# The second mixture's first product by Strassen's seven half products, over blocks of 768 tokens

## The chip, the cores and the metric

One core of a Trainium2 chip runs the whole program. The metric is the device time of one execution in microseconds (us), the median of several runs. TensorE (PE) multiplies and sums into PSUM, VectorE (DVE), ScalarE (ACT) and GpSimd (POOL) work elementwise, and SyncE (SP) issues most of the DMA transfers.

## What is computed

```python
x = attention(q, k, v, s)        # B=4, H=8, S=576, D=64, causal, with a cumulative bias -> 2304 tokens x 512
h = x @ w_in1;  x1 = (h * sigmoid(1.702 * h)) @ w_out1      # first mixture:  512 -> 2048 -> 512
h = x1 @ w_in2; r = maximum(h, 0)
out = (s2 * (r * r) + b2) @ w_out2                          # second mixture: 512 -> 2048 -> 512
```

All of it is float32. TensorE's float32 operands here are of the rounded kind (fp32r), so each product is made of three: an operand is split into a high part (a copy to fp32r) and a low part (the operand less its high part), and low x high, high x low and high x high are summed in PSUM.

## The kernel before

The 2048 hidden columns are 16 slices of 128, numbered f. Weights come from DRAM as pairs of 32-bit words, 512 KB for one f of `w_in` or `w_out` (`fetch_w`, the DMA at L125), are joined to floats (`join_w`: ACT at L139, DVE at L140 and L141) and split (`split_w`: ACT at L149, DVE at L150). The first part of the program runs the attention heads on TensorE among the first mixture's products (L404 for h, L444 for y), unit by unit; the first batch's attention heads run while the first mixture's weights are being loaded, and what order the vector engines take there is set by the scheduler of the language from the program's order and the buffers (only TensorE's order, and SP's in part, is written out by hand).

The last unit of the first mixture, 256 tokens, is `first_whole`: for each f twelve matmuls of 256 columns make h (L404), ACT, DVE, ACT and POOL turn it into two parts (L425, L426, L430, L431), and four f later twelve matmuls add them into four y sums (L580). Beside it the first weights of the second mixture are joined and split. `second` then goes over four blocks of 512 tokens and one of 256: for each f, `h2` sums twelve matmuls 128x512 (L554) in one PSUM bank, three banks in turn; ACT takes the positive part (L557), DVE squares it (L558) and applies s and b (L559), ACT makes the high part (L562), and the low part is made at L563 by POOL where f is even, by DVE where it is odd. Two f later (LEAD2) twelve matmuls at L604 add into four y sums, one for each 128 tokens. All weights of the second mixture stay in SBUF, split, after block 0 has brought them. `fetch_x` and `parts_x` load and split the tokens of a block (ACT at L544, POOL at L545) during the block ahead. In the second mixture the order of PE is by hand everywhere, that of ACT and DVE up to the end of block 0.

Of the kernel before, what the change touches and what calls it, by code (L numbers as in the profile page):

```python
# [17 lines left out]
P = 128  # L18
# [4 lines left out]
ACT, DVE = mybir.EngineType.Activation, mybir.EngineType.DVE  # L23
# [12 lines left out]
WIDE2, LEAD2, PLACES, FETCHED = 512, 2, 9, 5  # L36
# [31 lines left out]
def fused_kernel(ctx: ExitStack, tc: tile.TileContext, qkT, vP, s, w1i, w1o, w2i, w2o, s2, b2, out):  # L68
# [59 lines left out]
    def join_w(came):  # L128

        if came.dtype == F32:  # L130
            return came
        else:

            lower, upper = came[:, 0 : 2 * CM : 2], came[:, 1 : 2 * CM : 2]
            nc.scalar.activation(f32(upper), f32(upper), AF.Prelu, scale=2.0**-112, alpha=2.0**32)  # L139
            nc.vector.tensor_scalar(out=lower, in0=lower, scalar1=2.0**-29, scalar2=7.49, op0=ALU.mult, op1=ALU.min)  # L140
            nc.vector.scalar_tensor_tensor(  # L141
                out=lower, in0=upper, scalar=3, in1=lower, op0=ALU.logical_shift_left, op1=ALU.bitwise_or
            )
            return f32(lower)

    def split_w(single, tag, f):

        w = wp.tile([P, 2, CM], F32R, tag=tag, name=f"{tag}{f}")
        nc.scalar.activation(w[:, 0, :], single, AF.Copy)  # L149
        nc.vector.tensor_tensor(w[:, 1, :], single, f32(w[:, 0, :]), ALU.subtract)  # L150
        return w

    def load_w(stage, src, tag, f):
        return split_w(join_w(fetch_w(stage, src, f)), tag, f)


    with ExitStack() as p1:
        sp = p1.enter_context(tc.tile_pool(name="sp", bufs=8))
# [252 lines left out]
        def h_begin(ui, f, x):  # L411
            ph = begun[ui, f] = psM.tile([P, 512], F32, tag="m", name="ph1")
            for _ in h_sum(ph, units[ui].n, f, x, range(len(x))):
                pass

        def h_item(ui, f, x, between=None):
            n = units[ui].n
            if (ui, f) in begun:
                ph = begun.pop((ui, f))
                yield from h_sum(ph, n, f, x, range(NC - 1, NC))  # L420
            else:
                ph = psM.tile([P, 512], F32, tag="m", name="ph1")
                yield from h_sum(ph, n, f, x, range(NC))
# [72 lines left out]
        with tc.tile_pool(name="half0", bufs=1) as pool, tc.manual_schedule(engines={PE}):  # L496
            attention_pool(pool, B * H, 0)
            x0 = []
            with tc.manual_schedule(engines={PE, SP}):
                setup()  # L500
                for step in range(H + 2):
# [7 lines left out]
                    for f in range(len(wi), min(NF, 2 * step)):  # L509
                        wi[f] = load_w((wp, "wo", NF), w1i, "wi", f)  # L510
# [12 lines left out]
        with tc.tile_pool(name="half1", bufs=1) as pool, tc.manual_schedule(engines={PE}):  # L523
# [6 lines left out]
    rawp = ctx.enter_context(tc.tile_pool(name="rawp", bufs=PLACES))  # L530
    psY = ctx.enter_context(tc.tile_pool(name="psY", bufs=5, space=PSUM))
    xp2 = ctx.enter_context(tc.tile_pool(name="xp2", bufs=2))
    wi2, wo2 = {}, {}
    blocks = [(t, min(WIDE2, NT - t)) for t in range(0, NT, WIDE2)]

    def fetch_x(t0, n, cc):
        raw = xp2.tile([P, WIDE2], F32, tag="xraw2", name="xraw2")
        nc.sync.dma_start(raw[:, :n], x1_d[cc * P : (cc + 1) * P, t0 : t0 + n])
        return raw

    def parts_x(raw, n):

        x = rawp.tile([P, 2, WIDE2], F32R, tag="pair", name="xT2")
        nc.scalar.activation(x[:, 0, :n], raw[:, :n], AF.Copy)  # L544
        nc.gpsimd.tensor_tensor(x[:, 1, :n], raw[:, :n], f32(x[:, 0, :n]), ALU.subtract)  # L545
        return x

    def h2(f, x, n, g2, between):
        ph = psM.tile([P, 512], F32, tag="m", name="ph2")
        k = 0  # L550
        for cc in range(NC):
            wc = slice(cc * P, (cc + 1) * P)
            for a, b in ((1, 0), (0, 1), (0, 0)):
                nc.tensor.matmul(ph[:, :n], wi2[f][:, a, wc], x[cc][:, b, :n], start=(k == 0), stop=(k == 3 * NC - 1))  # L554
                k += 1
        r = xp.tile([P, 2 * NMAX], F32, tag="xT", name="r")[:, :n]
        nc.scalar.activation(r, ph[:, :n], AF.Relu)  # L557
        nc.vector.tensor_tensor(r, r, r, ALU.mult)  # L558
        nc.vector.tensor_scalar(out=r, in0=r, scalar1=s_sb, scalar2=b_sb, op0=ALU.mult, op1=ALU.add)  # L559
        between()  # L560
        g = [gp.tile([P, 2 * NMAX], F32R, tag="g", name="g2")[:, :n] for _ in range(2)]
        nc.scalar.activation(g[0], r, AF.Copy)  # L562
        (nc.vector if f % 2 else nc.gpsimd).tensor_tensor(g[1], r, f32(g[0]), ALU.subtract)  # L563
        g2[f] = g
# [28 lines left out]
    def second(t0, n, x, last):  # L593
        g2 = {}
        py = [psY.tile([P, C], F32, tag="y", name="py2") for _ in range(n // P)]
        for f in range(NF + LEAD2):
            if f < NF:
                h2(f, x, n, g2, join_next)
                yield f
            if f >= LEAD2:  # L600
                k = f - LEAD2
                for t in range(n // P):
                    for i, (a, b) in enumerate(((1, 0), (0, 1), (0, 0))):
                        nc.tensor.matmul(  # L604
                            py[t], g2[k][a][:, t * P : (t + 1) * P], wo2[k][:, b, :],
                            start=(k == 0 and i == 0), stop=(k == NF - 1 and i == 2),
                        )
        for t in range(n // P):
            y = xp2.tile([P, C], F32, tag="y2", name="y2", bufs=3)
            if last and t == n // P - 1:  # L610
                half = C // 2
                for i, (copy, queue) in enumerate(((nc.scalar.copy, nc.scalar), (nc.vector.tensor_copy, nc.sync))):
                    mine = slice(i * half, (i + 1) * half)
                    copy(y[:, mine], py[t][:, mine])
                    queue.dma_start(out[t0 + t * P : t0 + (t + 1) * P, mine], y[:, mine])
                continue
            if t % 2:
                nc.scalar.activation(y, py[t], AF.Copy)
            else:
                nc.vector.tensor_copy(y, py[t])  # L620
            nc.sync.dma_start(out[t0 + t * P : t0 + (t + 1) * P, :], y)

    order = sorted(
# [87 lines left out]
```

## Time and profile before

| | |
|---|---|
| runs | 1056.04, 1053.0, 1053.21 us; median 1053.21 us |
| profiled execution, span | 1052.8 us (its own time is not listed apart) |
| granted TensorE clock | 0.995 |
| PE busy | 1015.6 us, 96% of the span, 6216 matmuls |
| DVE / ACT / POOL busy | 650.6 / 535.8 / 347.7 us |

Busy time is the time in which an engine has an instruction running; a matmul's time in the trace is its own from start to end, and as matmuls overlap, the pace is read from a run of them (time divided by count). Idle time in square brackets stands before an instruction, with what released it. The program's stretches by time: attention and first mixture to 606 us, `first_whole` to 652 us, then blocks 0 to 4 of `second` from 652, 750, 837, 924 and 1011 us.

### The profile page before, as it was taken

To read this page: it belongs to the slowest core of one execution; us is meant where nothing else is said; L and a number is where in the kernel's file an instruction comes from. 1 tells how busy PE (TensorE), PEld (TensorE's weight loads), DVE (VectorE), ACT (ScalarE), POOL (GpSimd) and SP (SyncE) were. 2 spreads that over 40 slices of the span, in tenths; PEclk is the share of its full clock that TensorE was granted. 3 is DMA by queue.
4 is the path that set the end of the run, shared out by engine and by line. 5 is a ranking of instruction groups with operands and counts; after the bars stand their busy time and mean duration, and the time that the engine had idled before them with its cause. 6 is when DMAs were issued, how large, how long until landed. Compare 5 with 4: busy or idle time off the path is not lost.

```text
span 1052.8 us, 17330 instructions
## 1 busy us (share of the span) xinstructions
PE 1015.6 (96%) x6216; PEld 909.6 (86%) x6216; DVE 650.6 (62%) x1441; ACT 535.8 (51%) x1252; POOL 347.7 (33%) x382
## 2 busy tenths in 40 slices
PE   5989999999999999999999999999999999999998
PEld 3459989999989999999999999788888888888887
DVE  4689877567467788778877579866422332232343
ACT  4888856646536646656656557544422322222222
POOL 1126535435335436435445235112410301111011
PEclk9998999999999999999999999999999999999999
DMA  5665331221042232222222084531300100100010
GB/s 178 217 236 182 120 97 56 65 81 44 6 129 71 67 105 72 83 92 72 84 74 68 21 300 134 167 101 41 110 1 1 65 1 1 46 1 1 1 40 21
DMA packets 39181, 85.51 MB, mean 81 GB/s; under 512 B 5660, under 2 KB 16536, under 8 KB 39096
## 3 DMA queue, kind: packets, MB, share of 16 engines
q1 hardware_dynamic: 38888, 84.27, 25.1%
q8 instruction: 49, 0.80, 0.3%
q14 instruction: 36, 0.29, 0.1%
q10 hardware_dynamic: 208, 0.13, 0.0%
HBM read 70.29 MB, written 10.03 MB: 76 GB/s over the span
## 4 chain that ended last, share of the span: by engine, by line
PE 78%; DVE 11%; ACT 4%; DMA 3%; issue 2%; SPq 1%; DVEq 0%; ACTq 0%
PE py L604 19%; PE ph L554 18%; PE py L444 14%; PE ph L404 14%; PE ps L277 4%; PE pst L315 4%; PE po L342 3%; DVE hi L115 3%; DMA pair<-w1i 2%; DVE x L283 1%; PE py L580 1%; ACT x L289 1%; DVE pair L141 1%; DVE pair L140 1%; PE po L336 1%
## 5 line engine op out<-in xcount | busy, mean ns | idle before, releaser
L404 PE MATMUL ph<-xT,wi 128*128 128x320 f32 (+1 forms) x1536 | 246.1, 305 | 5.6 <-ACT xT L390 2.5
L404 PEld LDWEIGHTS ph<-xT,wi 128*128 128x128 f32 x1536 | 217.0, 193 | 7.1 <-ACT xT L390 3.0
L444 PE MATMUL py<-g,wo 128*128 128x320 f32 (+1 forms) x1344 | 215.2, 304 | 0.0
L604 PE MATMUL py<-wo,g 128*128 128x512 f32 x864 | 208.1, 390 | 2.4 <-POOL g L563 2.4
L554 PE MATMUL ph<-xT,wi 128*128 128x512 f32 (+1 forms) x960 | 208.4, 368 | 0.0
L554 PEld LDWEIGHTS ph<-xT,wi 128*128 128x128 f32 x960 | 169.0, 188 | 31.0
L604 PEld LDWEIGHTS py<-wo,g 128*128 128x128 f32 x864 | 161.1, 188 | 36.2 <-POOL g L563 3.3
L444 PEld LDWEIGHTS py<-g,wo 128*128 128x128 f32 x1344 | 188.0, 189 | 0.9 <-POOL g L431 0.2
L558 DVE TENSOR_TENSOR r<-r 128x512 f32<-128x512 f32 (+1 forms) x80 | 53.6, 670 | 189.1 <-ACT r L557 188.9
L431 POOL TENSOR_TENSOR g<-th,g 128x320 fp32r<-128x320 f32 (+1 forms) x128 | 116.3, 909 | 128.9 <-ACT g L430 114.2
L563 POOL TENSOR_TENSOR g<-r,g 128x512 fp32r<-128x512 f32 (+1 forms) x40 | 48.6, 1216 | 306.3 <-PE py L604 174.9
L289 ACT ACTIVATE x<-x,m 64x64 f32<-64x64 f32 (+2 forms) x160 | 89.5, 560 | 100.2 <-DVE m L283 98.8
L557 ACT ACTIVATE r<-ph 128x512 f32<-128x512 f32 (+1 forms) x80 | 44.4, 555 | 147.7 <-PE ph L554 146.1
L257 POOL TENSOR_TENSOR lo<-raw,hi 64x576 fp32r<-64x576 f32 (+1 forms) x56 | 68.1, 1217 | 123.0 <-issue 57.2
L283 DVE CUSTOM_DVE_ANT_0 x<-ps,mask 64x64 f32<-64x64 f32 (+2 forms) x160 | 68.1, 426 | 52.2 <-PE ps L277 50.4
L315 PE MATMUL pst<-ident,x 128*128 128x128 f32 (+2 forms) x480 | 85.8, 287 | 9.9 <-DVE ph L324 8.1
L562 ACT ACTIVATE g<-r 128x512 fp32r<-128x512 f32 (+1 forms) x80 | 47.1, 589 | 91.9 <-DVE r L559 91.8
L113 POOL TENSOR_SCALAR x<-x,tot 64x64 f32<-64x64 f32 (+1 forms) x96 | 49.3, 520 | 91.3 <-DVE tot L294 71.4
L321 ACT ACTIVATE ph<-pst 64x256 fp32r<-64x256 f32 (+2 forms) x144 | 67.0, 473 | 20.6 <-PE pst L315 19.2
L315 PEld LDWEIGHTS pst<-ident,x 128*128 128x128 f32 (+2 forms) x480 | 54.8, 136 | 24.7 <-DVE ph L324 13.0
L425 ACT ACTIVATE th<-ph 128x320 f32<-128x320 f32 (+1 forms) x128 | 51.7, 404 | 45.5 <-PE ph L404 42.7
L426 DVE SCALAR_TENSOR_TENSOR th<-th,ph 128x320 f32<-128x320 f32 (+1 forms) x128 | 57.5, 449 | 22.5 <-ACT th L425 21.5
(71 smaller groups left out, 1334.8 us busy)
## 6 DMA issues: line engine op xcount, KB each, us to landing
raw<-qkT SPq DMA_DIRECT2D x32, 416.0 KB
pair<-w1o SPq DMA_DIRECT2D x16, 512.0 KB
pair<-w1i SPq DMA_DIRECT2D x16, 512.0 KB
pair<-w2i SPq DMA_DIRECT2D x16, 512.0 KB
pair<-w2o SPq DMA_DIRECT2D x16, 512.0 KB
raw<-qkT SPq DMA_DIRECT2D x24, 320.0 KB
vraw<-vP SPq DMA_DIRECT2D x16, 320.0 KB
out<-y SPq DMA_DIRECT2D x17, 256.0 KB
```

The costliest lines, as they stand in the source:

```text
L257: nc.gpsimd.tensor_tensor(lo[:D, kc], raw[:D, kc], f32(hi[:D, kc]), ALU.subtract)
L283: nc.vector.tensor_tensor_reduce(out=x[:w, j0:j1], in0=ps[:w, : j1 - j0], in1=mask[:w, WIDE - a0 + j0 : WIDE - a0 + j1], scale=-1.0 / ROOT ...
L289: nc.scalar.activation(x[:w, :a1], x[:w, :a1], AF.Exp, bias=least, scale=-1.0, accum_out=tot[:w, c : c + 1])
L315: nc.tensor.transpose(ps[: j1 - j0, at : at + a1 - a0], t["x"][c][: a1 - a0, j0:j1], ident[: a1 - a0, : a1 - a0])
L321: nc.scalar.activation(t["ph"][:rows, base:end], ps[:rows, :m], AF.Copy)
L404: nc.tensor.matmul(ph[:, :n], wi[f][:, a, cc * P : (cc + 1) * P], x[cc][:, b, :n], start=(k == 0), stop=(k == 3 * NC - 1),)
L426: nc.vector.scalar_tensor_tensor(out=th[:, :n], in0=th[:, :n], scalar=1.0, in1=ph[:, :n], op0=ALU.add, op1=ALU.mult)
L431: nc.gpsimd.tensor_tensor(g[:, 1, :n], th[:, :n], f32(g[:, 0, :n]), ALU.subtract)
L444: nc.tensor.matmul(py[:, :n], wo[f][:, a, wc], g_t[ui, f][:, b, :n], start=(k == 0), stop=(k == 3 * G - 1))
L554: nc.tensor.matmul(ph[:, :n], wi2[f][:, a, wc], x[cc][:, b, :n], start=(k == 0), stop=(k == 3 * NC - 1))
L558: nc.vector.tensor_tensor(r, r, r, ALU.mult)
L604: nc.tensor.matmul(py[t], g2[k][a][:, t * P : (t + 1) * P], wo2[k][:, b, :], start=(k == 0 and i == 0), stop=(k == NF - 1 and i == 2),)
```

## The change

The second mixture takes its tokens in three blocks of 768 (two halves of 384, `HALF2`), and its first product by Strassen's scheme for 2 x 2 blocks. The blocks of the weights are `w_in2` for one pair of slices (f even, f odd) by two halves of the 512 inputs, those of the tokens two halves of the inputs by two halves of the block. Seven half products take the place of eight: each is 6 matmuls of 128 x 384 (two 128-deep slices of inputs, three terms each). A step p is one pair of slices, so a block has 8 steps.

The work around it:
- `product` (L687) sums into three banks. Slots 0, 2, 4 and 5 of a step add one after another into one bank, `sum_p`, and ACT copies the partial sum out (`taken`, L735) after slots 0, 2, 4 and 5 before the next of them goes on. Slot 1 has the bank `sum_q`, slots 3 and 6 have `sum_r`. DVE adds the copies to `sum_q` and `sum_r` as it reads them (`added`, L738). `squared` (DVE, L741, 768 columns), `affine` and `high` (ACT, L744 and L748) and `low` (L751, DVE for even f, POOL for odd f) make the two parts.
- y of a step is 36 matmuls of 512 columns (L702), which stand 5 or 6 at a time behind each slot, from step 1's slot 3 on (`LAG2`).
- The weight blocks: POOL forms the sums of a pair (`sums_of`, L604, four operations of 256 columns), ACT and DVE split the operands (`parts_of`, L620 and L621: three of 512 and one of 256 columns). Block 0 writes these parts, 1.83 MB for a step, to DRAM (L622), and blocks 1 and 2 read them back (L614).
- The tokens: DVE forms differences (L641, L642) and ACT with DVE or POOL splits them (L647, L648); a table, `X_WORK`, sets beside which slot. For block 0 this stands in the loop around `first_whole`.
- The order of PE, ACT, DVE and POOL is by hand from `first_whole` to the end. Buffers of `wp` have a tag each, and the pool ranges of the attention lie on the other side of SBUF.

```diff
+    N2, W = HALF2, 2 * P
+    NP, T2, N_BLOCKS = NF // 2, 2 * HALF2 // P, NT // (2 * HALF2)
+    parts_d = dram.tile([NP, 4, P, 4 * W], F32, name="parts_d")
...
+    def sums_of(p):
+        w, t = whole[p], wp.tile([P, 4, W], F32, tag="wi7", name="sums")
+        a11, a12, a21, a22 = (w[:, f, k * W : (k + 1) * W] for f in range(2) for k in range(2))
+        for to, a, b, op in (
+            (t[:, 1], a21, a22, ALU.add), (t[:, 0], t[:, 1], a11, ALU.subtract),
+            (t[:, 2], a11, a21, ALU.subtract), (t[:, 3], a12, t[:, 0], ALU.subtract),
+        ):
+            nc.gpsimd.tensor_tensor(to, a, b, op)
...
+    def parts_of(p, k, first):
...
+        if not first:
+            nc.sync.dma_start(flat, kept)
+            return
...
+        nc.scalar.activation(t[:, 0, :], src, AF.Copy)
+        nc.vector.tensor_tensor(t[:, 1, :], src, f32(t[:, 0, :]), ALU.subtract)
+        nc.sync.dma_start(kept, flat)
...
-    def second(t0, n, x, last):
...
+    PRODUCTS = (
+        ("p", 0, 0, "11"), ("q", 0, 1, "21"), ("p", 1, 0, "2"), ("r", 1, 1, "1"),
+        ("p", 2, 0, "3"), ("p", 3, 0, "4"), ("r", 2, 1, "22"),
     )
+    def product(ps, p, slot, x):
+        _, group, at, kind = PRODUCTS[slot]
+        w, first = parts[p, group], slot in (0, 1, 3)
+        for k in range(6):
+            a, b = ((1, 0), (0, 1), (0, 0))[k % 3]
+            c0 = at * W + k // 3 * P
+            nc.tensor.matmul(
+                ps[:, :N2], w[:, a, c0 : c0 + P], x[kind, k // 3][:, b, :], start=(first and k == 0), stop=(k == 5),
+                skip_group_check=not first,
+            )
...
+            for slot, (bank, _, _, _) in enumerate(PRODUCTS):
+                if slot in (0, 1, 3):
+                    ps[bank] = psM.tile([P, 512], F32, tag="m0" if slot == 0 else "m1", name="sum_" + bank)
+                product(ps[bank], p, slot, x)
+                if slot == 0:
+                    taken(e[0], "p")
...
+                elif slot == 1:
+                    added(even[:, :N2], "q", e[0])
...
+                elif slot == 4:
+                    taken(e[2], "p")
+                    added(odd[:, N2:], "r", e[2])
+                elif slot == 5:
+                    taken(odd[:, :N2], "p")
+                elif slot == 6:
+                    squared(odd)
+                    added(even[:, N2:], "r", e[1])
...
+                beside(p, slot)
+                if step > 1 or (step == 1 and slot >= LAG2):
+                    y_next(6 if slot == 4 else 5)
```

The order of TensorE changes only from the end of `first_whole` on. There it was, before, twelve matmuls for each f (`ph` is the sum of one f, `py` a sum of y):

```order
L554 MATMUL ph_8892<-xT_8644,wi_8362 128x512 x3
L554 MATMUL ph_8892<-xT_8647,wi_8362 128x512 x3
L554 MATMUL ph_8892<-xT_8732,wi_8362 128x512 x3
L554 MATMUL ph_8892<-xT_8735,wi_8362 128x512 x3
L604 MATMUL py_8830<-wo_8401,g_8855 128x512
L604 MATMUL py_8830<-wo_8401,g_8854 128x512 x2
L604 MATMUL py_8831<-wo_8401,g_8855 128x512
```

And it is now, from step 1's slot 2 to the y matmuls behind its slot 5:

```order
L687 MATMUL sum_p<-xs,part 128x384 x6
L687 MATMUL sum_r<-xs,part 128x384 x6
L702 MATMUL py_8988<-wo_8495,g_8913 128x512 x3
L702 MATMUL py_8988<-wo_8454,g_8953 128x512 x2
L687 MATMUL sum_p<-xs,part 128x384 x6
L702 MATMUL py_8988<-wo_8454,g_8953 128x512
L702 MATMUL py_9013<-wo_8495,g_8913 128x512 x3
L702 MATMUL py_9013<-wo_8454,g_8953 128x512 x2
L687 MATMUL sum_p<-xs,part 128x384 x6
L702 MATMUL py_9013<-wo_8454,g_8953 128x512
L702 MATMUL py_9033<-wo_8495,g_8913 128x512 x3
L702 MATMUL py_9033<-wo_8454,g_8953 128x512
```

On TensorE step 0 and step 1's slots 0 to 2 have no y matmuls between them; later each slot has five or six behind it.

The first eleven rows of DVE's step 2, in block 0, as they now stand ( `whole` is a pair of weight slices, `part` its split operands, `g` the parts of the hidden values):

```order
L738 TENSOR_TENSOR even<-sum_q,e 128x384
L154 TENSOR_SCALAR pair<-pair 128x512
L156 SCALAR_TENSOR_TENSOR whole<-pair 128x512
L621 TENSOR_TENSOR part<-whole,part 128x512
L751 TENSOR_TENSOR g_9099<-even,g_9099 128x768
L621 TENSOR_TENSOR part<-sums,part 128x512
L154 TENSOR_SCALAR pair<-pair 128x512
L156 SCALAR_TENSOR_TENSOR pair<-pair 128x512
L738 TENSOR_TENSOR odd<-sum_r,e 128x384
L165 TENSOR_TENSOR wo_9159<-pair,wo_9159 128x512
L621 TENSOR_TENSOR part<-sums,part 128x512
```

The whole step has 20 DVE operations: four joins of two operations each, two `wo` splits, four part splits (three of 512 columns, one of 256), three `added`, two `squared` and one `low`; POOL has four `sums_of` operations of 256 columns and one `low` of 768.

The other place is far ahead of the change, in the first batch's attention, where the scheduler sets the order. SP's transfers stood there so (`w1i` and `w1o` are the first mixture's weights, 512 KB each; `raw` and `vraw` belong to the attention heads):

```order
L125 DMA pair<-w1i 128x1024 x2
L237 DMA raw<-qkT 64x640
L233 DMA raw<-rows_d 4x320
L234 DMA raw<-rows_d 4x320
L244 DMA vraw<-vP 128x384
L125 DMA pair<-w1i 128x1024 x2
```

And now:

```order
L133 DMA pair<-w1i 128x1024 x2
L254 DMA raw<-qkT 64x640
L250 DMA raw<-rows_d 4x320
L251 DMA raw<-rows_d 4x320
L133 DMA pair<-w1o 128x1024 x3
L261 DMA vraw<-vP 128x384
L133 DMA pair<-w1i 128x1024 x2
```

Seven `w1o` slices are loaded, joined and split ahead of most of the attention heads of the first batch, between them, where they came behind before. TensorE's own order in this stretch is the same. DVE there, before and now, at the same place (L283 and L300 are the same mask operation of a head):

```order
L141 SCALAR_TENSOR_TENSOR pair<-pair 128x512
L283 ISA x,m<-ps,mask 128x320
L283 ISA m 128x1
L140 TENSOR_SCALAR pair<-pair 128x512
L150 TENSOR_TENSOR wi_280<-pair,wi_280 128x512
L141 SCALAR_TENSOR_TENSOR pair<-pair 128x512
```

```order
L165 TENSOR_TENSOR wo_689<-pair,wo_689 128x512
L300 ISA x,m<-ps,mask 128x320
L300 ISA m 128x1
L154 TENSOR_SCALAR pair<-pair 128x512
L156 SCALAR_TENSOR_TENSOR pair<-pair 128x512
L165 TENSOR_TENSOR wi_280<-pair,wi_280 128x512
```

A `wo` split has come in ahead of the head's mask operation, and six more follow within the next hundred rows.

## Rows read from the trace of the kernel before

**Rows 1.** The page: busy us (share) x instructions; chain by engine.
```profile
PE 1015.6 (96%) x6216; PEld 909.6 (86%) x6216; DVE 650.6 (62%) x1441; ACT 535.8 (51%) x1252; POOL 347.7 (33%) x382
...
PE 78%; DVE 11%; ACT 4%; DMA 3%; issue 2%; SPq 1%; DVEq 0%; ACTq 0%
```

**Rows 2.** Chain of waits in order of time: start us, duration us, what.
```profile
613.57 1.44 PE py L580 x12
...
668.50 2.72 PE py L604 x12
671.22 2.72 PE ph L554 x12
```

**Rows 3.** Lines by form: xcount | busy us, mean ns | idle us before, releasers.
```profile
L604 PE MATMUL py<-wo,g 128*128 128x512 f32 x864 | 208.1, 390 | 2.4 <-POOL g L563 2.4
L554 PE MATMUL ph<-xT,wi 128*128 128x512 f32 x768 | 183.2, 389 | 0.0
...
L139 ACT ACTIVATE pair<-pair 128x512 f32<-128x512 f32 x64 | 43.3, 676 | 5.6 <-DMA pair<-w1i 4.9 <-DMA pair<-w1o 0.4
...
L557 ACT ACTIVATE r<-ph 128x512 f32<-128x512 f32 x64 | 38.3, 598 | 131.4 <-PE ph L554 130.0 <-POOL xT L545 1.2
...
L554 PE MATMUL ph<-xT,wi 128*128 128x256 f32 x192 | 25.2, 283 | 0.0
```

**Rows 4.** Windows: length, busy of PE, PEld, DVE, ACT, POOL; PEclk, DMA share, GB/s.
```profile
600.00:629.40 29.40, 29.40 (x248) 29.40 (x247) 18.32 (x34) 15.21 (x35) 8.97 (x9) 1.00 0.74 265
629.40:666.00 36.60, 34.48 (x243) 32.17 (x242) 34.23 (x50) 24.30 (x48) 16.14 (x12) 1.00 0.53 171
640.00:652.80 12.80, 12.80 (x107) 12.71 (x107) 12.20 (x15) 9.14 (x18) 9.86 (x7) 1.00 0.46 143
666.00:750.00 84.00, 84.00 (x373) 69.36 (x371) 54.20 (x82) 39.56 (x68) 20.99 (x16) 1.00 0.31 96
750.00:837.00 87.00, 87.00 (x384) 71.87 (x384) 31.01 (x44) 23.51 (x39) 18.18 (x14) 1.00 0.09 28
```

**Rows 5.** Timeline of PE at the start of the second mixture.
```profile
652.29 8.35 PE L554 MATMUL ph<-xT,wi 128*128 128x512 f32 x36
662.76 3.02 PE L604 MATMUL py<-wo,g 128*128 128x512 f32 x12 [2.12 <-POOL g L563]
```

**Rows 6.** Timeline of DVE, last third of `first_whole`.
```profile
640.35 0.42 DVE L140 TENSOR_SCALAR pair<-pair 128x512 uint32<-128x512 uint32 x1
640.88 0.70 DVE L141 SCALAR_TENSOR_TENSOR pair<-pair 128x512 uint32<-128x512 uint32 x1
...
642.89 0.42 DVE L426 SCALAR_TENSOR_TENSOR th<-th,ph 128x256 f32<-128x256 f32 x1 [0.17 <-ACT th L425]
...
644.27 1.59 DVE L141 SCALAR_TENSOR_TENSOR pair<-pair 128x512 uint32<-128x512 uint32 x1
...
652.70 0.68 DVE L150 TENSOR_TENSOR wi<-pair,wi 128x512 fp32r<-128x512 f32 x1
```

**Rows 7.** Timeline of POOL in `first_whole`.
```profile
612.16 0.74 POOL L431 TENSOR_TENSOR g<-th,g 128x256 fp32r<-128x256 f32 x1 [0.70 <-PE ph L404]
```

**Rows 8.** Timeline of block 1: a POOL and a DVE operation together.
```profile
755.81 1.29 POOL L563 TENSOR_TENSOR g<-r,g 128x512 fp32r<-128x512 f32 x1 [2.53 <-PE ph L554]
756.36 1.29 DVE L558 TENSOR_TENSOR r<-r 128x512 f32<-128x512 f32 x1 [1.35 <-ACT r L557]
```

**Rows 9.** Windows of the first batch's attention, and right behind it.
```profile
20.00:70.00 50.00, 47.63 (x141) 25.71 (x141) 37.11 (x99) 41.73 (x101) 10.00 (x15) 1.00 0.71 231
70.00:102.00 32.00, 27.57 (x156) 25.66 (x155) 30.87 (x72) 28.04 (x69) 14.99 (x17) 0.84 0.58 199
```

**Rows 10.** Window of ten us behind it.
```profile
80.00:90.00 10.00, 10.00 (x68) 9.72 (x68) 9.94 (x24) 8.97 (x23) 7.82 (x8) 0.94 0.62 206
```

**Rows 11.** Timeline of PE there: idle time and its releaser.
```profile
73.97 0.41 PE L404 MATMUL ph<-xT,wi 128*128 128x320 f32 x1 [2.14 <-ACT xT L390]
...
93.89 0.85 PE L404 MATMUL ph<-xT,wi 128*128 128x320 f32 x4 [1.89 <-DVE th L426]
```

More of the change, by code (lines that the diff above doesn't have):

```diff
@@ L22 @@
 PE, SP = mybir.EngineType.PE, mybir.EngineType.SP
-ACT, DVE = mybir.EngineType.Activation, mybir.EngineType.DVE
+ACT, DVE, POOL = mybir.EngineType.Activation, mybir.EngineType.DVE, mybir.EngineType.Pool
 BUFS = (
@@ L493, in run @@
                 attend(item)
[L496 removed]
+        with tc.tile_pool(name="half0", bufs=1, side="right") as pool, tc.manual_schedule(engines={PE}):
             attention_pool(pool, B * H, 0)
@@ L541, in parts_x @@
[L541 to L564, printed above, removed]
@@ new lines, in join_next, with split_next @@
+    def join_next():
+        sign_next()
+        merge_next()
+    def split_next():
+        if n_split[0] < len(joined):
+            tag, f = order[n_split[0]]
+            if tag == "wo":
+                wo2[f] = split_w(joined[n_split[0]], "wo", f)
+            n_split[0] += 1
+    sums, parts = {}, {}
+    n_parts = [0]
+    def sums_of(p):
[6 more added lines that the diff above has]
+            nc.gpsimd.tensor_tensor(to, a, b, op)
+        sums[p] = t
@@ L591, in first_whole @@
             nc.sync.dma_start(x1_d[c * P : (c + 1) * P, t0_of[ui] : t0_of[ui] + n], y[:, :n])
-    def second(t0, n, x, last):
[L594 to L621, printed above, removed]
@@ new lines, in y_of, with one @@
+    def y_of(block, p, g2):
+        def one(t, k):
+            if p == 0 and k == 0:
+                pool, tag = (psY, y_tags[t]) if y_tags[t] else (psM, "m2")
+                y_sums[t] = pool.tile([P, C], F32, tag=tag, name="py2")
+            f, (a, b) = 1 - k // 3, ((1, 0), (0, 1), (0, 0))[k % 3]
+            nc.tensor.matmul(
+                y_sums[t], g2[f][:, a, t * P : (t + 1) * P], wo2[2 * p + f][:, b, :],
+                start=(p == 0 and k == 0), stop=(p == NP - 1 and k == 5),
+            )
+            if p == NP - 1 and k == 5:
+                y_out(block, t, y_sums[t])
+        todo.extend((one, t, k) for t in range(T2) for k in range(6))
@@ new lines, in y_next, with y_out @@
+    def y_next(n):
+        for one, t, k in todo[:n]:
+            one(t, k)
+        del todo[:n]
+    def y_out(block, t, sums):
+        row = block * 2 * N2 + t * P
+        y = wp.tile([P, 2 * CM], F32, tag=f"wi{t % 3}", name="y2")[:, :C]
+        if block == N_BLOCKS - 1 and t == T2 - 1:
+            half = C // 2
+            for i, (copy, queue) in enumerate(((nc.scalar.copy, nc.scalar), (nc.vector.tensor_copy, nc.sync))):
+                mine = slice(i * half, (i + 1) * half)
+                copy(y[:, mine], sums[:, mine])
+                queue.dma_start(out[row : row + P, mine], y[:, mine])
+            return
+        if t % 2:
+            nc.scalar.activation(y, sums, AF.Copy)
+        else:
+            nc.vector.tensor_copy(y, sums)
+        nc.sync.dma_start(out[row : row + P, :], y)
```

297 lines of the change are left out of this document (223 added, 74 removed).

## The prediction

> **What bounds the kernel now.** I read the page first, then the chain of waits, the lines by form, windows by stage, and last the timelines at the places where work is added. The page says that TensorE is busy for 96% of the span and that the chain of waits runs through it for 78% [rows 1]. The first product of the second mixture never makes TensorE wait (idle 0.0), the second one 2.4 us in all [rows 3], of which 2.1 stand at one place, where y of the first f waits for POOL's low part [rows 5]. In the windows TensorE is busy for 87.00 of block 1's 87.00 us, while DVE has 31.0, ACT 23.5 and POOL 18.2 [rows 4]. So in the second mixture TensorE's pace is the time, and the vector engines have room. That does not hold at its start: between 629.4 and 666 us DVE is busy for 34.2 of 36.6 us and POOL for 16.1 [rows 4].
>
> **TensorE's saving.** Twelve matmuls of 512 columns take 2.72 us, twelve of 256 take 1.44 [rows 2]: 0.2267 and 0.120 us each. No row has 384 columns there; the middle of the two is 0.1733, and since both ends are paces of the same loops I take it without a range. Before, the first product has 768 matmuls of 512 columns and 192 of 256 [rows 3]: 174.1 + 23.0 = 197.1 us. Now it is 3 blocks x 8 steps x 42 = 1008 matmuls of 384 columns: 174.7 us. The second product keeps its 864 matmuls. Term: **-22.4 us**. A step is 42 x 0.1733 + 36 x 0.2267 = 15.44 us of TensorE.
>
> **Partial sums read between accumulations.** ACT must have read `sum_p` before the next slot adds to it. The reading is 0.60 us for 512 columns [rows 3], less for 384. Between slots 0 and 2, and 2 and 4, lies a whole other slot (1.04 us) and ten y matmuls; between 4 and 5 only six y matmuls, 1.36 us. That covers the reading. Without the y matmuls, in step 0, only the 0.6 us at slot 4 is bare. I take nothing for it beyond what the next term holds.
>
> **Blocks 1 and 2.** Per step of 15.44 us DVE has three additions (0.55 each), two squares and a low part (0.94 each), 4.5 us; ACT four readings and four operations of 768 columns, some 6 us. The parts come back from DRAM, 1.83 MB a step, 119 GB/s, where the loads around 600 to 629 us run at 265 GB/s [rows 4]. Nothing is bare there: 0.
>
> **The start and block 0.** Here the vector work grows, and POOL and DVE do not run freely side by side. One row shows it: POOL's 512-column operation runs from 755.81 for 1.29 us, and DVE's square, started at 756.36, takes 1.29 [rows 8], where a 512-column operation on DVE otherwise takes 0.68 [rows 6]. The reading of PSUM at L426 stays at 0.42, while a join is stretched from 0.70 to 1.59 [rows 6]. To price this I add up a stretch. From 640.0 to 652.7 DVE does three L426, four joins and three splits, alone 3 x 0.42 + 4 x 1.12 + 3 x 0.68 = 7.8 us; POOL three operations of 256 columns (0.74 alone, [rows 7]) and four of 512 (1.29), 7.4. These 15.2 us took 12.7, a factor of **0.84**, with 12.20 us of DVE shown busy [rows 4].
>
> For the change I count both from f = 10 of `first_whole` (from there on the new operand work is due) to the first y matmul in step 1. DVE: ten operations of 256 columns (0.42), nine joins (1.12), ten of 512 (0.68), twenty of 384 (0.55, the middle) and three of 768 (0.94, by the same slope): 34.9 us. POOL: fourteen of 256 (0.74), six of 384 (1.01) and one of 768 (1.84): 18.3. Together 53.2, at 0.84 it is 44.7 us. TensorE has in the same stretch six f of 24 and four of 12 matmuls at 0.120, then 60 at 0.1733: 33.5 us. So it waits 11.2 us; the 2.1 of before go with it. Term: **+9.1 us**. Bounds: 33.5 if both ran freely (DVE's 34.9 alone nearly fits, so -1), and 53.2 if nothing overlaps (+17.6).
>
> In steps 2 to 5 and parts of 1 and 6, about five steps, weights still come: DVE 12.8 us (twenty operations), POOL 4.8, together 17.6, at 0.84 it is 14.8, under 15.44. Term: 0, with 5 x 2.2 = 11 at full serialisation.
>
> [...]
>
> **The order far ahead.** In the first batch's attention seven `w1o` slices are now joined and split before TensorE starts the first mixture. DVE gets 7 x (1.12 + 0.68) = 12.6 us more in the stretch of 20 to 70 us, ACT 7 x 2 x 0.68 = 9.5 [rows 3, 6]. They have 37.1 and 41.7 of 50 now [rows 9], so ACT would need 51.2, and at the densest share of the neighbouring window, 0.9 [rows 10], 56.9 us: 6.9 later. SP's queue issues these loads ahead of the heads' operands; they are part of that delay. Behind it, from 70 to 102 us, TensorE is idle for 4.4 us, waiting for ACT and DVE [rows 11], and works at a granted clock of 0.84 [rows 9], which costs another 4.4; the seven slices no longer burden that stretch, and I let half of the 8.8 come back. Term: **+2.5 us**, between -2 and +7.
>
> **Sum.** Against the profiled span: 1052.8 - 22.4 + 9.1 + 2.5 = 1042.0; that span lies 0.4 under the median of 1053.2, so **1042.4 us**. A change of 0.3% (3.2 us) is about what a measurement of this kernel can tell.
>
> **Rivals.**
> - *All of it is hidden* (0.24). If the new operand work is begun early enough, or DVE and POOL overlap more than in my stretch, the start costs nothing: 1053.2 - 22.4 - 2.1 = 1028.7, with the order far ahead 1031. For it: before f = 10, from 600 to 629 us, DVE is busy for only 18.3 of 29.4 us [rows 4]. Against: the tokens' differences need the rows of x1 and the first weight pair, and the operations stand in one order on each engine.
> - [...] With a factor k for the overlap the time is 1031.2 + (53.2 k - 33.5), plus 5 x (17.6 k - 15.44) once k is above 0.88. Fully serial, k = 1: 1061.7. It is slower than before (over 1056.4) from k = 0.962, and no gain (1050) from 0.917. For it: the 1.59 join and the 1.29 square; waits of DVE for ACT's high parts and POOL's for DVE's joins add idle time that my stretch has little of. Against: the same mix of operations made 0.84 there.
> - *TensorE waits for the partial sums* (0.05). If the six y matmuls do not cover the reading at slot 4 (ACT late behind other work), each of 24 steps waits about 0.6: +14, 1057. Against: ACT has the most room of all in these stages. [...]
> - *Block 0's transfers are late* (0.06). Two pairs of weights of each kind (2.1 MB) and the parts written (1.83 MB) make 3.9 MB a step, 255 GB/s, near the 265 of [rows 4]. At the 231 of [rows 9] a step takes 17.0: 5 x 1.6 = +8, 1050.
>
> **Chances and range.** The forecast has 0.48 (1034 to 1050). Faster: all of the first rival (0.24), 0.45 of the forecast's and half of the transfers' (0.03): 0.72. Slower: 0.13 of the port's 0.17 and 0.03 of the partial sums': 0.16. The rest, 0.12, is within 0.3%. The range goes from the first rival's 1029 to 1057, leaving out about 0.07 below (a gain far ahead on top of it) and 0.13 above.
>
> **What would show it.** Right: blocks 1 and 2 at 8 x 15.44 = 123.5 us each with TensorE busy throughout; matmul runs of L687 at 0.173 us each; idle time of TensorE between 629 and about 690 us of some 11 us, released by DVE or POOL; in block 0's middle steps DVE busy nearly all the time and TensorE still without idle time; the first mixture's first product (L421) begun some us later than L404 was. Wrong: idle before L687 in blocks 1 and 2 released by ACT's reading (third rival), steps of block 0 over 16 us with DVE always busy (second), idle released by transfers of `part` or `pair` (fourth), or no idle at the start at all (first).

## The result and the profile after

The change made the kernel slower: 1061.27 us (median of 4 runs, 1059.7 to 1063.41) against 1054.62 for the kernel before in the same comparison, a ratio of 1.0061 with a 95% interval of 1.0039 to 1.0082. 1042.4 was forecast, a gain of 1%. The profiled execution spans 1057.9 us, 5.1 more than the one of before.

The page shows TensorE with less work and a smaller share of the chain of waits [rows 1]:

```profile
PE 1001.6 (95%) x6264; PEld 918.2 (87%) x6264; DVE 677.0 (64%) x1453; ACT 590.3 (56%) x1322; POOL 369.0 (35%) x392
...
PE 70%; DVE 14%; ACT 7%; DMA 4%; issue 4%; SPq 1%; DVEq 0%; ACTq 0%
```

In the lines by form the first product now waits, and so does y; before they had 0.0 and 2.4 us of idle time [rows 3]:

```profile
L702 PE MATMUL py<-wo,g 128*128 128x512 f32 x864 | 226.7, 394 | 4.0 <-DVE g L751 4.0
...
L687 PE MATMUL sum_p<-xs,part 128*128 128x384 f32 x576 | 118.0, 341 | 8.2 <-ACT e L735 8.2
```

All of this waiting lies at the start of the second mixture and in its block 0. TensorE's timeline there (start, duration, instruction, idle time before it with its releaser), where before it was one wait of 2.12 us [rows 5]:

```profile
657.46 1.58 PE L662 MATMUL py<-g,wo 128*128 128x256 f32 x11 [0.56 <-POOL g L448]
658.87 1.22 PE L687 MATMUL sum_p<-xs,part 128*128 128x384 f32 x6
659.93 1.20 PE L687 MATMUL sum_q<-xs,part 128*128 128x384 f32 x6
667.56 2.29 PE L687 MATMUL sum_p<-xs,part 128*128 128x384 f32 x6 [6.43 <-ACT e L735]
...
673.22 1.33 PE L687 MATMUL sum_p<-xs,part 128*128 128x384 f32 x6 [0.58 <-ACT e L735]
...
677.75 1.31 PE L687 MATMUL sum_q<-xs,part 128*128 128x384 f32 x6 [1.09 <-DVE even L738]
680.24 1.31 PE L687 MATMUL sum_p<-xs,part 128*128 128x384 f32 x6 [1.17 <-ACT e L735]
682.53 1.31 PE L687 MATMUL sum_r<-xs,part 128*128 128x384 f32 x6 [0.98 <-DVE even L738]
686.62 0.72 PE L702 MATMUL py<-wo,g 128*128 128x512 f32 x2 [2.08 <-DVE g L751]
...
703.06 0.73 PE L702 MATMUL py<-wo,g 128*128 128x512 f32 x2 [0.47 <-DVE g L751]
...
719.54 0.73 PE L702 MATMUL py<-wo,g 128*128 128x512 f32 x2 [0.49 <-DVE g L751]
```

After 752.45 us, in step 5 of block 0, there is no wait at all, and a step is 15.70 us, from one slot 0 to the next:

```profile
901.24 1.22 PE L687 MATMUL sum_p<-xs,part 128*128 128x384 f32 x6
902.30 1.32 PE L702 MATMUL py<-wo,g 128*128 128x512 f32 x5
903.46 1.21 PE L687 MATMUL sum_q<-xs,part 128*128 128x384 f32 x6
...
916.94 1.22 PE L687 MATMUL sum_p<-xs,part 128*128 128x384 f32 x6
```

Far ahead, the first mixture's first product begins at 71.67 us; the same 27 matmuls stood at 65.09 before, and the wait behind them has grown from 2.14 to 2.91 us [rows 11]. Before and now:

```profile
65.09 5.27 PE L404 MATMUL ph<-xT,wi 128*128 128x320 f32 x27
```

```profile
71.67 5.23 PE L421 MATMUL ph<-xT,wi 128*128 128x320 f32 x27
...
81.29 0.64 PE L421 MATMUL ph<-xT,wi 128*128 128x320 f32 x1 [2.91 <-ACT xT L407]
```

So the 5.1 us of the spans come from three places. The second mixture starts at 658.87 where it started at 652.29 [rows 5]: +6.6. Of this 5.8 is there when `first_whole` begins (611.98 for 606.21), and 0.8 is lost in its last y matmuls, which wait 0.56 us for POOL. The second mixture's 24 steps take 24 x 15.70 = 376.8 us of TensorE; before, the 400.5 us from 652.29 to the end held 2.4 us of waits and about 3.8 of tail, so 394.3: -17.5. The waits: from 658.87 to step 1's slot 4 at 687.18 go 28.3 us for 12.8 us of matmuls (66 at 0.177, as from 658.87 to 659.93, and five of y), 15.5 lost, and four steps of 16.46 in place of 15.70 lose 3.0 more: 18.5, less the 2.4 of before, +16.1. The sum is +5.2.

### The profile page after: what moved, and what is told of

It reads as the page before. It is cut to its first block, busy times and chain, and to the rows that moved or that the text cites. A ratio compares the mean times of both kernels' runs of the same rounds, so it can differ in the third digit from the quotient of the medians.

```text
span 1057.9 us, 17742 instructions
## 1 busy us (share of the span) xinstructions
PE 1001.6 (95%) x6264; PEld 918.2 (87%) x6264; DVE 677.0 (64%) x1453; ACT 590.3 (56%) x1322; POOL 369.0 (35%) x392
## 4 chain that ended last, share of the span: by engine, by line
PE 70%; DVE 14%; ACT 7%; DMA 4%; issue 4%; SPq 1%; DVEq 0%; ACTq 0%
PE py L702 16%; PE py L461 14%; PE ph L421 13%; PE sum_p L687 8%; PE ps L294 5%; PE pst L332 4%; PE sum_r L687 4%; DVE hi L123 3%; PE po L359 3%; DMA pair<-w1i 2%; PE sum_q L687 2%; DVE x L300 1%; DVE part L621 1%; DMA pair<-w1o 1%; ACT x L306 1%
## 5 line engine op out<-in xcount | busy, mean ns | idle before, releaser
L702 PE MATMUL py<-wo,g 128*128 128x512 f32 x864 | 226.7, 394 | 4.0 <-DVE g L751 4.0
L421 PEld LDWEIGHTS ph<-xT,wi 128*128 128x128 f32 x1536 | 215.8, 192 | 8.2 <-ACT xT L407 3.8
L702 PEld LDWEIGHTS py<-wo,g 128*128 128x128 f32 x864 | 159.8, 188 | 29.9 <-DVE g L751 6.2
L448 POOL TENSOR_TENSOR g<-th,g 128x320 fp32r<-128x320 f32 (+1 forms) x128 | 113.7, 889 | 128.6 <-ACT g L447 117.0
L751 POOL TENSOR_TENSOR g<-odd,g 128x768 fp32r<-128x768 f32 x24 | 47.1, 1962 | 287.4 <-ACT g L748 287.4
L687 PE MATMUL sum_p<-xs,part 128*128 128x384 f32 x576 | 118.0, 341 | 8.2 <-ACT e L735 8.2
L687 PEld LDWEIGHTS sum_p<-xs,part 128*128 128x128 f32 x576 | 104.0, 189 | 16.8 <-ACT e L735 9.1
L300 DVE CUSTOM_DVE_ANT_0 x<-ps,mask 64x64 f32<-64x64 f32 (+2 forms) x160 | 68.1, 426 | 54.9 <-PE ps L294 52.8
L735 ACT ACTIVATE e<-sum_p 128x384 f32<-128x384 f32 x72 | 35.3, 490 | 117.7 <-PE sum_p L687 117.6
L447 ACT ACTIVATE g<-th 128x320 fp32r<-128x320 f32 (+1 forms) x128 | 56.3, 440 | 34.3 <-DVE th L443 33.5
L123 DVE TENSOR_SCALAR hi<-raw 128x832 fp32r<-128x832 f32 (+1 forms) x48 | 69.9, 1456 | 2.1 <-DMA raw<-qkT 2.0
```

The source lines that it names most:

```text
L123: nc.vector.tensor_scalar(out=out, in0=in_, scalar1=scale, scalar2=None, op0=ALU.mult)
L300: nc.vector.tensor_tensor_reduce(out=x[:w, j0:j1], in0=ps[:w, : j1 - j0], in1=mask[:w, WIDE - a0 + j0 : WIDE - a0 + j1], scale=-1.0 / ROOT ...
L421: nc.tensor.matmul(ph[:, :n], wi[f][:, a, cc * P : (cc + 1) * P], x[cc][:, b, :n], start=(k == 0), stop=(k == 3 * NC - 1),)
L448: nc.gpsimd.tensor_tensor(g[:, 1, :n], th[:, :n], f32(g[:, 0, :n]), ALU.subtract)
L687: nc.tensor.matmul(ps[:, :N2], w[:, a, c0 : c0 + P], x[kind, k // 3][:, b, :], start=(first and k == 0), stop=(k == 5), skip_group_check=n ...
L702: nc.tensor.matmul(y_sums[t], g2[f][:, a, t * P : (t + 1) * P], wo2[2 * p + f][:, b, :], start=(p == 0 and k == 0), stop=(p == NP - 1 and ...
```

## The experiments

**1. The staging slots reversed.** The idea to be tried is that the order far ahead comes from the buffers: with a tag each, a split `w1o` slice needs only that one buffer free in which one `w1i` slice was staged. With the staging slots reversed, the first `w1o` slice gets its buffer last.

```diff
-                        wi[f] = load_w((wp, f"wo{f}", 1), w1i, "wi", f)
+                        wi[f] = load_w((wp, f"wo{NF - 1 - f}", 1), w1i, "wi", f)
```

> The changed kernel, with the first mixture's staging slots taken in reverse order, so that a w1o slice finds no free slot before the last w1i slice is joined; the scheduler then places the w1o loads and splits as in the kernel before. Theory (the order far ahead costs what the trace shows, 658.87 against 652.29 us for the start of the second mixture, and nothing of it comes back): the first L421 matmul back at about 65 us, the second mixture begun at 652 to 653, the time 6 us shorter than the change's 1061.3, so 1055. Rival (the delay is covered: the second mixture's start waits for its vector work anyway): the start stays late in another place and the time falls by under 2 us, to about 1060.

Measured: 1.0048 of before (1.0033 to 1.0064); the interval overlaps the change's, so no gain is shown. The first product does begin earlier, but the `w1o` splits now come among the first hidden values, and it waits there:

```profile
66.52 5.95 PE L421 MATMUL ph<-xT,wi 128*128 128x320 f32 x27
...
94.59 2.02 PE L421 MATMUL ph<-xT,wi 128*128 128x320 f32 x12 [1.50 <-DVE th L443]
99.36 0.86 PE L421 MATMUL ph<-xT,wi 128*128 128x320 f32 x4 [2.65 <-DVE th L443]
```

The second mixture starts at 660.5, later still. This neither confirms the theory nor the rival: the edit made another order, not the old one.

**2. The tags alone, in the kernel before.**

```diff
-    wp = ctx.enter_context(tc.tile_pool(name="wp", bufs=NF))
+    wp = ctx.enter_context(tc.tile_pool(name="wp", bufs=1))
...
-        w = wp.tile([P, 2, CM], F32R, tag=tag, name=f"{tag}{f}")
+        w = wp.tile([P, 2, CM], F32R, tag=f"{tag}{f}", name=f"{tag}{f}")
...
-                        wi[f] = load_w((wp, "wo", NF), w1i, "wi", f)
+                        wi[f] = load_w((wp, f"wo{f}", 1), w1i, "wi", f)
```

> The kernel before, with nothing of the change but a tag for each weight buffer in place of one rotating ring of 16. Theory (the tags alone move the w1o loads ahead and cost 6 us): second mixture begun at about 658, time about 1060. Rival (the delay comes from the change's other edits, the sides of SBUF or the longer program): within 1 us of before, 1054.

Measured: 1.0040 (1.0026 to 1.0055), some 4 us, with the same order of every engine far ahead as in the change. The theory holds; in time the size is nearer 4 than 6. In the profiled execution the second mixture begins late, as in the change:

```profile
659.46 8.35 PE L554 MATMUL ph<-xT,wi 128*128 128x512 f32 x36
```

**3. Without the second pair's sums on POOL.** Here is what they meet in the change, on POOL, DVE and ACT:

```profile
657.45 2.54 POOL L648 TENSOR_TENSOR xs<-raw,xs 128x384 fp32r<-128x384 f32 x2
659.94 1.05 POOL L604 TENSOR_TENSOR sums<-whole 128x256 f32<-128x256 f32 x1
661.07 0.92 POOL L604 TENSOR_TENSOR sums<-sums,whole 128x256 f32<-128x256 f32 x1
```

```profile
656.73 3.67 DVE L648 TENSOR_TENSOR xs<-diff,xs 128x384 fp32r<-128x384 f32 x3
660.32 1.09 DVE L641 TENSOR_TENSOR diff<-raw 128x384 f32<-128x384 f32 x1
...
664.49 0.55 DVE L641 TENSOR_TENSOR diff<-raw,raw 128x384 f32<-128x384 f32 x1
```

```profile
662.44 0.94 ACT L647 ACTIVATE xs<-diff 128x384 fp32r<-128x384 f32 x2 [4.24 <-DVE diff L642]
...
667.01 0.49 ACT L735 ACTIVATE e<-sum_p 128x384 f32<-128x384 f32 x1
```

The difference at 660.32 takes 1.09 us beside POOL and 0.55 at 664.49 without it. And ACT, which could read the first partial sum when slot 0 ends at about 660, does it at 667.01: in its queue splits stand ahead that wait for DVE's differences (4.24 us at 662.44).

```diff
-            if f in (10, 17):
-                sums_of(0 if f == 10 else 1)
+            if f == 10:
+                sums_of(0)
+            if f == 17:
+                sums[1] = sums[0]
```

> The changed kernel without the four POOL operations that form the weight sums of step 1's pair at the end of the first mixture; the split reads the sums of pair 0 in their place, so this part of the computation is left out. In the trace POOL does them from 659.94 to 663.68 while DVE's differences and splits take 1.09, 0.96 and 1.57 in place of 0.55, 0.55 and 1.02. Theory (DVE is slowed by POOL's operations): TensorE's wait before step 0's slot 2 falls from 6.4 us by about 1.5 to 2.5, and the time with it. Rival (DVE's own queue is the limit): the wait stays within 0.5 us of 6.4.

Measured: 1.0036 (1.0023 to 1.0049), with an interval that overlaps the change's. The wait itself fell by 1.5 us:

```profile
666.35 2.29 PE L687 MATMUL sum_p<-xs,part 128*128 128x384 f32 x6 [4.94 <-ACT e L735]
```

So these four operations of POOL cost a quarter of this wait. It is not POOL's whole share: its two token splits from 657.45 on stayed in, and while they ran, three of DVE's splits took 3.67 us (656.73), where two of the same kind took 1.01 with POOL idle (666.03). How much of the wait these two are was not tried.

**4. The low part one slot earlier.** On DVE the even slice's low part came behind a join and a part split that belong to the next step:

```profile
681.93 0.55 DVE L738 TENSOR_TENSOR even<-sum_q,e 128x384 f32<-128x384 f32 x1
682.40 0.49 DVE L154 TENSOR_SCALAR pair<-pair 128x512 uint32<-128x512 uint32 x1
682.99 1.04 DVE L156 SCALAR_TENSOR_TENSOR whole<-pair 128x512 uint32<-128x512 uint32 x1
683.95 1.22 DVE L621 TENSOR_TENSOR part<-whole,part 128x512 fp32r<-128x512 f32 x1
685.09 1.47 DVE L751 TENSOR_TENSOR g<-even,g 128x768 fp32r<-128x768 f32 x1
```

```diff
                     if before:
                         high(*before, 0)
+                        low(*before, 0, nc.vector)
                 elif slot == 2:
                     taken(e[1], "p")
-                    if before:
-                        low(*before, 0, nc.vector)
```

> The changed kernel with DVE's low part of the even slice issued one slot earlier, ahead of the join and the part split that stand before it now. Theory (in block 0 each step waits for this operation because of its place on DVE, 0.47 to 0.49 us idle and a step of 16.46 us against 15.70): the steps of block 0 fall to about 15.7 and the time by 3 to 5 us, to about 1057. Rival (DVE has too much to do in block 0 in any order): the wait moves to another operation, DVE additions or part splits, and the time stays within 1 us.

Measured: 0.9997 (0.9985 to 1.0009), against the change's 1.0061: 6.8 us by the middles, 3.2 at the nearest ends. The trace accounts for 5.1, the 2.08 of step 1 and the 3.0 of the four steps. A step of block 0 is 15.70 us, or 15.92 for one, with no idle time:

```profile
687.51 1.21 PE L687 MATMUL sum_p<-xs,part 128*128 128x384 f32 x6
...
703.21 1.22 PE L687 MATMUL sum_p<-xs,part 128*128 128x384 f32 x6
...
719.13 1.21 PE L687 MATMUL sum_p<-xs,part 128*128 128x384 f32 x6
```

The windows say how near to full DVE is there, of the change and then of this run (length, busy of PE, PEld, DVE, ACT, POOL):

```profile
703.63:753.00 49.37, 47.92 (x235) 42.19 (x234) 44.53 (x61) 32.98 (x56) 19.22 (x15) 1.00 0.69 232
```

```profile
703.21:753.00 49.79, 49.79 (x248) 44.52 (x247) 48.16 (x67) 34.32 (x58) 20.87 (x16) 1.00 0.73 239
```

DVE is busy for 97% of the time, where the change had 90%, with TensorE at 100%. The work fits; its place in the queue was the cost.

**5. One ring for staging and `wo`,** as before the change, which gives PE, DVE, ACT and POOL the old order up to `first_whole`.

```diff
-        w = wp.tile([P, 2, CM], F32R, tag=f"{tag}{f}", name=f"{tag}{f}")
+        ring = dict(tag="wo", bufs=NF) if tag == "wo" else dict(tag=f"{tag}{f}")
+        w = wp.tile([P, 2, CM], F32R, name=f"{tag}{f}", **ring)
...
-                        wi[f] = load_w((wp, f"wo{f}", 1), w1i, "wi", f)
+                        wi[f] = load_w((wp, "wo", NF), w1i, "wi", f)
...
-        tokens = [Tokens(0, [f"wo{2 + cc}" for cc in range(NC)])]
+        tokens = [Tokens(0, ["wo"] * NC)]
```

> The changed kernel with one ring of 16 buffers for the first mixture's staging and w1o (and for the second mixture's wo and block 0's raw tokens), as in the kernel before, in place of a tag each. With it the order of every engine ahead of the second mixture is the kernel before's, row by row; the earlier try, which took the staging slots in reverse, had moved the w1o splits behind the first hidden values instead, and lost by 110 us what it had won by 66. Theory (the tags cost 6 us far ahead and nothing else does): first mixture begun at about 65, second at 652 to 653 us, time 5 to 6 us under the change's, so within 1 us of before. Rival (the second mixture's start is waited for anyway): second mixture begun at 652 but its first wait longer, time under 2 us less than the change's.

("110" and "66" in this text are places on the time axis.) Measured: 0.9986 (0.9972 to 1.0000) against 1.0061, some 8 us by the middles and 4 at the nearest ends. The first product begins at 65.90 us; the waits of the second mixture are the change's, only earlier, so the rival falls:

```profile
664.87 2.29 PE L688 MATMUL sum_p<-xs,part 128*128 128x384 f32 x6 [6.43 <-ACT e L736]
```

**6. Both repairs** (the diffs of 4 and 5 together).

> Both repairs together: the ring of the run beside it, and DVE's low part of the even slice one slot earlier, which alone took some 5 us off. Theory (the two costs lie in different stretches and add): 10 to 11 us under the change, about 0.995 of the kernel before. Rival (one hides the other): no better than the better of the two alone.

Measured: 0.9951 (0.9930 to 0.9972), 1.1% under the change, some 11.6 us; the two alone come to 6.8 and 7.9 by their middles. Within the intervals they add.

**7. y in groups of twelve,** on top of both repairs.

```diff
-                    y_next(6 if slot == 4 else 5)
+                    y_next(12 if slot in (1, 4, 6) else 0)
```

> As the run with both repairs, but the y matmuls stand in three groups of twelve behind slots 1, 4 and 6 instead of seven groups of five or six: 6 changes between the two products in a step in place of 14. A step of blocks 1 and 2 took 15.70 us where 42 x 0.1733 + 36 x 0.2267 is 15.44. Theory A (each change between the products costs some 10 to 18 ns): a step falls by 0.08 to 0.15 us. Theory B (a 384-column matmul itself takes 0.1767 or more, as in step 0 where nothing stands between): the step stays within 0.04 us of 15.70 apart from what A takes, at 42 x 0.1767 + 36 x 0.2267 = 15.58 or more. Blocks 1 and 2 should show no idle time of TensorE if the reading of the partial sums is covered by one other slot.

Measured: 0.9922 (0.9897 to 0.9948), 3.1 us under the two repairs by the middles, though the intervals overlap; what shows the effect is the step. It runs from 902.08 to 917.66, 15.58 us in place of 15.70:

```profile
902.08 1.21 PE L688 MATMUL sum_p<-xs,part 128*128 128x384 f32 x6
903.12 1.20 PE L688 MATMUL sum_r<-xs,part 128*128 128x384 f32 x6
904.16 2.93 PE L703 MATMUL py<-wo,g 128*128 128x512 f32 x12
906.93 1.21 PE L688 MATMUL sum_p<-xs,part 128*128 128x384 f32 x6
...
917.66 1.21 PE L688 MATMUL sum_p<-xs,part 128*128 128x384 f32 x6
```

Six matmuls of 384 columns take 1.04 us here (902.08 to 903.12), the 0.1733 each that I took; twelve of 512 columns with a change on either side take 2.77 (from 904.16 to the next slot at 906.93), 0.05 over 2.72. So it is the change between the streams that costs: (15.58 - 15.44) / 6 = 23 ns each here, (15.70 - 15.44) / 14 = 19 ns there. Theory A holds: 15.58 is also what theory B named, but B rests on 0.1767 for a 384-column matmul, and they take 0.1733 here. Between the two products of before, both of 512 columns, a change cost nothing (2.72 for either twelve [rows 2]), so in these runs the cost came with the change of length. And no wait shows where only one other slot covers the reading of a partial sum.

**8. Tokens and weights earlier,** on top of both repairs: one more staging buffer in the last free space, the tokens fetched two f earlier and their work of f = 11 to 18 done at f = 8 to 15.

```diff
-            if 6 <= f < 6 + NC:
-                x.fetch(f - 6)
-            if f in (10, 17):
-                sums_of(0 if f == 10 else 1)
+            if 4 <= f < 4 + NC:
+                x.fetch(f - 4)
+            if f in (8, 15):
+                sums_of(0 if f == 8 else 1)
...
-            elif f == 13:
+            elif f == 10:
                 x.diff(0, 0, nc.vector)
```

> As the run with both repairs, with the token and weight work around the end of the first mixture begun earlier: one more staging buffer, tokens fetched two f earlier, their differences and splits three f earlier, the sums of pair 0 two and of pair 1 two f earlier. Theory (DVE's and POOL's volume between f = 10 and step 1 is the wait, and DVE is idle for 22 of the 35 us before f = 10): the wait before step 0's slot 2 (6.4 us) falls to 1 to 3 and the time by 3 to 5 us against the run with both repairs. Rival (the wait is of order, not of volume, or it moves into the first mixture, whose hidden values then come late): the sum of TensorE's idle time from 630 to 690 us stays within 1 us.

Measured: 0.9919 (0.9896 to 0.9943), 3.4 us under the two repairs by the middles, though the intervals overlap. The wait before slot 2 is gone, but part of it has gone into the first mixture's last y:

```profile
651.49 0.38 PE L666 MATMUL py<-g,wo 128*128 128x256 f32 x1 [1.48 <-ACT g L448]
...
655.24 0.39 PE L666 MATMUL py<-g,wo 128*128 128x256 f32 x1 [1.36 <-ACT g L448]
...
661.57 1.22 PE L691 MATMUL sum_p<-xs,part 128*128 128x384 f32 x6
...
665.79 1.32 PE L691 MATMUL sum_p<-xs,part 128*128 128x384 f32 x6 [0.88 <-ACT e L739]
```

All of TensorE's waits from 640 to 690 us add up to 8.3 us, where the run with both repairs has 10.9. Of both theories something is true: 6.4 us less before slot 2, but only 2.5 less in all.

**9. Both of these together.**

> The two gains on top of both repairs together: token and weight work begun earlier, and y in groups of twelve. They lie in different stretches (the start of the second mixture, and its pace), so if the account is right they add: some 4 to 5 us for the start and 24 x 0.12 = 3 us for the pace against the run with both repairs, that is about 0.988 of the kernel before. If the longer stretches of products without y between them uncover the waits of the start again, no better than the earlier work alone.

Measured: 0.9898 (0.9881 to 0.9916), 1045.09 us against 1056.5 for the kernel before. It beats both kernels, and by its interval the two repairs as well: 5.6 us by the middles, where the two gains were 3.1 and 3.4. Its interval overlaps those of runs 7 and 8, so that they add is likely and not shown. This is the gain that was forecast (1042.4 of 1053.2), but with four edits that the forecast did not have.

**10. The order of the wait alone,** on top of both repairs.

```diff
-            if k is not None and (p > 0 or k > 1):
+            if k is not None:
...
-            if f > 17:
-                parts_of(1, f - 18, True)
...
-            elif f == 18:
-                x.split("3", 1, nc.vector)
-                x.split("4", 1, nc.vector)
...
+                    if (p, slot) in ((0, 1), (0, 2)):
+                        x.split("34"[slot - 1], 1, nc.vector)
```

> As the run with both repairs, but with two token splits (for slots 4 and 5) and two part splits of step 1 moved from the end of the first mixture to behind slots 1 and 2 of step 0; no work is left out or added. In the trace ACT's reading of the first partial sum stands behind the high parts of these splits, which wait for DVE's differences. Theory A (the wait before slot 2 is the place in ACT's and DVE's queues): it falls from 6.4 to 3 to 4 us, and the time by 2 us or more. Theory B (volume: DVE has all of this to do before the first y): the wait before slot 2 falls but comes back before later slots of steps 0 and 1, the sum of idle time from 650 to 690 us stays within 1 us of 10.9, and so does the time.

Measured: 0.9937 (0.9920 to 0.9954), 1.5 us under the two repairs by the middles, though the intervals overlap.

```profile
657.15 2.29 PE L688 MATMUL sum_p<-xs,part 128*128 128x384 f32 x6 [3.23 <-ACT e L736]
...
664.82 1.33 PE L688 MATMUL sum_p<-xs,part 128*128 128x384 f32 x6 [1.18 <-ACT e L736]
```

The wait fell by 3.2 us and 0.6 came back before slot 5; all waits together are 8.2 us in place of 10.9. For the wait that is theory A: half of it was four splits' place in the queue. For the time it is not shown: theory A named 2 us or more, and 1.5 with overlapping intervals came.

## Why the prediction was wrong

The forecast was 1042.0 on the profiled span; it came out at 1057.9. Of the 15.9 us between them 4.9 are TensorE's saving, 3.3 the order far ahead, 4.8 the start and 3.0 block 0's steps (rounded, 16.0). By the steps of the prediction:

- **TensorE's saving, -22.4: measured -17.5.** The count and the 0.1733 us of a 384-column matmul were right. The step of 15.44 us left out that each step now changes fourteen times between streams of 384 and 512 columns, at some 20 ns each: 15.70 us, 24 x 0.26 = 6.2 us. The kernel before was itself 1.3 us above the sum of its paces, so 4.9 is the difference. Run 7 shows it.
- **The order far ahead, +2.5: measured +5.8.** The delay of the first product was foreseen (6.9, measured 6.6). What failed is "I let half of the 8.8 come back": 0.8 came back, not 4.4. The 32 us from 76.5 on, the place of 70 to 102 before, lose 7.9 us (4.9 of waits, 3.0 by a granted clock of 0.89) where they lost 8.8, though DVE is now busy for 26.3 of them and not 30.9. So most of the loss of [rows 9, 11] had not come from the seven slices. Runs 2 and 5 put the cost of the tags at some 4 and 8 us by the middles of their intervals.
- **The start, +9.1: measured +13.9 (15.5 and 0.8, less the 2.4 of before); the mechanism was half of it.** I priced the vector work as a volume, 53.2 us at a factor of 0.84. The stretch from f = 10, at 635.3, to the y matmuls that wait for the first low part, at 686.6, took 51.3 us and not 44.7 (length, busy of PE, PEld, DVE, ACT, POOL):

```profile
635.30:686.60 51.30, 38.43 (x260) 36.15 (x259) 44.47 (x64) 30.90 (x63) 28.66 (x26) 0.93 0.59 197
```

  DVE is busy for 44.5 us of it, about what the sum gave; the 6.8 us over are gaps in which DVE itself waits, 5.8 of them for ACT. The factor came from a stretch in which DVE had almost no gaps. (The sum had two counts short, too, which move its term by some 1.5 us: 66 matmuls and not 60 stand ahead of the first y, and four more of POOL's sums fall into the stretch, 681.4 to 685.8.) From 655 to 668 DVE works with one gap of 0.6, so volume is there. The sum left out two things. One is the place in the queue: ACT's reading stood behind splits from the end of slot 0 at about 660 to 667.01 (run 10, 3.2 us of the 6.4), and the low part behind a join and a part split (run 4, 2.08 us at step 1). The other is TensorE's granted clock: after the wait of 6.43 us it was 0.52 from 667.5 to 671.4, so that slots 2 and 3 took 3.87 us in place of 2.1.
- **Block 0's steps, 0: measured +3.0, for the same reason.** "17.6 at 0.84 is 14.8, under 15.44" was right as a volume, as run 4 shows (97% of DVE, no wait), but four steps waited for the place of one operation.
- **Blocks 1 and 2, and the partial sums: right about the waits.** There is no idle time (a block takes 125.6 us, for the 20 ns above, and not 123.5), and the reading is covered by six y matmuls or one slot; the bare one in step 0 costs 0.58 us, where 0.6 was said.

Of the rivals, the second, whose 0.17 stands in the chances as the port's, gave the time (1061.7), not the cause. No run shows a port. What the traces show is that some operations of DVE took longer with POOL at work: the difference begun at 660.32, with POOL at work since 659.94 and until 660.99, took 1.09 us, and the one at 664.49, with POOL idle, 0.55. Such stretching was in the factor of 0.84, too; four operations of POOL are 1.5 us of the 6.4 in run 3, and at the start it may be more. The rival's own sign, steps over 16 us with DVE always busy, is half there: they are 16.46 us, but DVE has a tenth of them free, and with the same work in another order they are 15.70. That rival had named one thing that did come, the idle time of DVE behind ACT's high parts (5.1 of the 5.8 us above). But taken for the whole it would have been the right time for a wrong reason, as the two repairs together (run 6) win back some 11.6 us with no operation of DVE or POOL left out.

Not settled: how much of run 8's gain is order and how much is volume, how much of the start's wait is POOL's, and whether run 2 and run 5 really differ on the tags (their intervals overlap). The profiles of runs 5, 6, 7 and 10, with one and the same order ahead, begin the second mixture between 651.7 and 656.2 us, so a single profile tells the delay there only to some us. But the groups do not mix: with the order of before (652.3, and these four) the mean is 653.4, with the tags' order (the change and runs 2, 3 and 4, 658.9 to 661.9) it is 659.9.

## What to carry to other kernels

Adding up what an engine has to do tells whether it fits, not when the one result comes that another engine waits for: for each such wait list what stands ahead of that result in the engine's queue (here splits stood ahead of a reading by ACT until 667.01, where slot 0 had ended at about 660), and put the operations that release TensorE ahead of those that only prepare a later step (run 4: steps of 15.70 us in place of 16.46). An edit of buffer tags can move instructions far from the place it is made for; compare each engine's order over the whole program, and undo the moves before the edit itself is judged. A scheme that saves an eighth of the columns pays in smaller pieces, so count the changes between streams, too (here fourteen a step, at some 20 ns each).

## What was not expected of the hardware

A change between a run of 384-column and one of 512-column matmuls cost about 20 ns here (19 and 23 by the two groupings), though six of 384 columns behind one another take 1.04 us and twelve of 512 take 2.72. A wait of 6.4 us was followed by a granted clock of 0.52 over the next 3.9 us, which added 1.8 us to it. The length of the wait does not tell how slow the matmuls behind it are: the first y matmuls of the second mixture waited 2.12 us in the kernel before and 2.11 in run 2, and the same twelve then took 3.02 us [rows 5] at a granted clock of 1.00 in the one and 4.61 in the other:

```profile
669.92 4.61 PE L604 MATMUL py<-wo,g 128*128 128x512 f32 x12 [2.11 <-POOL g L563]
```
